# Attention and MoE on one core: two pairs of token blocks merged in the first product, w_out's landing places changed, a new written-out order

## The chip, the cores and the metric

The kernel runs on one core of a Trainium2 chip. The metric is the device time of one execution in microseconds (us). A core has five engines that run side by side, each working through its own list of instructions in order and waiting on semaphores where it needs another's result: PE (TensorE, matrix products; PEld is its loading of the stationary operand), DVE (VectorE), ACT (ScalarE), POOL (GpSimd) and SP (SyncE, which here issues the DMAs).

## The reference

```
scores = (q @ k.T) / sqrt(64)          # 4 batches, 12 heads, 448 tokens, 64 wide
attn   = softmax(causal mask(scores))  # rows divided by (sum + 1e-9)
x      = (attn @ v)                    # back to 1792 tokens x 768
h      = x @ w_in                      # 768 x 2048
g      = h * (1 / (1 + exp(-1.702 * h)))
out    = g @ w_out                     # 2048 x 768, float32
```

## The kernel before

**Numbers.** Large products are not done in float32. Each operand is split into a high and a low float16 part (`split`; `scaled` writes the high part and `rest` the low one) and three of the four products are summed: high x high, high x low, low x high. Splitting is the work of ACT and DVE. The weights arrive as int32 words and are brought to float32 first (`to_f32`), scaled by a factor from the largest sum of squares (`gram` on PE, then `gram_max`, `all_sum`, `norm_scale`), and then split. The attention of the first two groups is done in float32 (`plain=2`), that of the others in split float16.

**Blocks.** Tokens are worked in chunks of 64 columns. `TUNE["groups"]` cuts the batches into nine blocks, here numbered 0 to 8: batch 0 chunks 0-4, batch 1 chunks 0-3, batch 2 chunks 0-4 and 4-7, batch 3 chunks 0-4 and 4-7, batch 1 chunks 3-5 and 5-7, batch 0 chunks 4-7. The widths are 256, 192, 256, 192, 256, 192, 128, 128 and 192 columns. For a block and each of six head pairs u, `unit` does scores, masked exponentials (`chunk`, a custom DVE instruction), the split of p, a transposition by DMA, and the product with v, whose result lands in xT.

**The MoE of a block.** `moe(n)` follows the attention of the next block. `h_slice` computes the eight slices of w_in (256 of its 2048 columns each) for the block; both 128-column halves t of a slice share one PSUM bank, so a block may be 256 columns wide. Each slice is four PE operations of 18 matmuls (line 410, helper `halves`: a product is two matmuls of 64 weight columns that run beside each other in the array). ACT takes tanh (line 1401), DVE forms the gelu (line 1406), and gT gets the high and low parts (lines 468 and 473). `out_tile` multiplies two chunks of gT with w_out (line 1442), in two halves nh of 384 columns and eight operations of 12 matmuls each. xT and gT are rings of seven chunks.

**The weights.** w_in lands in eight slices in `wob`, whose space is later w_out's. `w_out_load` brings the 16 blocks of w_out; a block's int32 words first land in a buffer that is named in `TUNE["raw"]`: K0 is K's own staging buffer `kk`, V0 that of v (`vraw`), P0 that of p, and W11, W13, W15 are parts of `wob`.

**The order.** Nothing is scheduled at run time. Every operation is registered in `Ops.add` with the engines that may do it, and the string `ORDER` lists all of them by number and engine (S, P, A, D, G). An engine executes its operations in the order of that string, SP its DMAs too. The string is the output of a planner that worked with the cost figures in the `add` calls; those figures have no other use in the kernel.

```
    for n, (b, c0, c1, gr) in enumerate(blocks):
        ...
        if n:
            moe(n - 1)
    moe(NB - 1)
```

Of the kernel before, what the change touches and what calls it, by code (L numbers as in the profile page):

```python
# [26 lines left out]
    raw=(['W11', 'K0', 'V0', 'P0', 'W13', 'W15', 'K0', 'P0'], ['W11', 'W13', 'W15', 'V0', 'K0', 'P0', 'V0', 'P0']),  # L27
# [22 lines left out]
    wi2=2.63,  # L50
    parts=(((0, 1), (1, 3), (3, 6)), ((0, 3), (3, 6))),
# [3 lines left out]
1D 3G 2A 60S 0G 4S 45S 57S 9S 541G 14S 108S 61P 49S 5A 62A 6D 7A 84P 27S 8D 47S 58P 85A 59A 111S 10D 82P 491S 11A  # L55
46S 70P 12A 83D 13D 15A 159S 63P 71D 162S 73D 16A 109P 64D 447S 66D 74A 17D 93P 444S 72A 110D 65A 18D 86P 67A 75P
77D 96D 19P 28A 78D 94D 32S 87D 133P 89D 97A 20D 29D 79P 48S 95A 76D 21P 68P 88A 112P 22D 90A 30D 80A 98P 24D 100D
23D 113A 31D 134A 432S 121P 69A 101D 25A 99D 135P 122D 114P 124D 50S 91P 136D 123A 160P 115D 117D 125A 144P 26D 118A
436S 116A 137P 161A 163P 92A 102P 145D 164A 215S 147D 184P 146A 140D 210S 128D 148A 186P 138D 494S 129D 185D 141A
119P 103D 434S 172P 33A 187D 165P 139A 34D 81P 538S 173D 35A 168D 126P 166D 433S 175D 188P 169A 151D 120D 195P 167A  # L60
36D 174A 437S 51P 176A 191D 189D 152D 127A 196D 104P 198D 192A 52D 37P 190A 179D 228S 105D 197A 573S 53P 130P 216D
199A 545S 448P 54D 38D 217A 180D 202D 445P 56D 55D 131D 39P 149P 617D 40D 449D 106A 153P 218D 446A 42D 469P 107D
211A 142P 203D 450P 219D 150A 233S 467P 143A 435S 132P 212D 154A 470A 451D 155P 43A 213D 453D 170P 214D 177P 468A
457P 156D 452A 181P 251S 171A 41D 44D 178A 471P 193P 157A 200P 182A 454A 495P 458D 229A 204P 158D 246S 478P 194A
472D 492P 474D 459A 230D 183P 201A 479D 220P 205A 462D 231D 496A 493A 626D 324S 206P 463D 473A 232D 480A 497P 475A
504P 207D 552A 514P 221D 455P 500D 234A 498D 222P 483D 516P 505D 264S 484D 438P 223D 515A 456D 208A 235D 460P 225D
517A 439D 618P 236D 226A 209D 518P 336S 237D 440P 619P 461A 252A 224D 227D 238P 499A 501A 464P 247A 269S 525P 620P
253D 465A 635D 506A 521D 254D 476P 522A 248D 621P 553A 255D 477A 330S 325A 627P 239D 249D 622A 441D 481P 519D 250D
520A 240P 539P 482A 628P 265A 287S 443D 509D 526D 510D 241D 623D 527A 574P 629P 540A 266D 624A 243D 242D 530D 267D
244A 256P 282S 625D 630P 268D 575A 337A 485P 257D 245D 466P 631A 258P 576P 300S 487P 270A 636P 632D 486A 271A 259D  # L70
577D 502P 261D 644D 488D 637P 633A 544S 579D 272D 262A 593P 634D 638P 273D 503A 645P 288A 263D 305S 578A 639P 594A
489A 260D 274P 580A 289D 640A 531D 490D 507P 283A 646P 275D 641D 508A 290D 276P 331A 595P 284D 511P 291D 647P 301A
285D 642A 583P 277D 512A 302D 648P 596A 326A 286D 523P 643D 597P 649A 292P 279D 524A 303D 551A 654P 327D 280A 293D
304D 294P 528P 513P 295D 328D 306A 655P 297D 281D 529A 354S 298A 532P 534P 656P 307D 533A 550A 299D 581P 308A 657P
582A 338A 309D 318S 332A 278D 584D 310P 339D 585A 650D 604P 333A 311D 586P 340D 312P 651A 313D 598D 587A 588D 360S
600D 355A 315D 589D 535D 590P 652D 316A 653D 605D 663P 662D 334D 599A 601A 317D 393S 591A 319A 602P 658A 664P 320D
606A 342S 659D 603A 348S 536A 321D 607P 356A 665P 609D 296D 537D 777S 322D 660A 592P 361A 666P 661D 375S 608A 357D
362A 323P 610D 672P 671D 314D 358D 667A 611P 363D 394A 399S 673P 668D 612A 442D 680D 364D 613P 669A 674P 343A 670D
405S 329P 986D 344A 614D 675P 371D 372D 615A 349D 681P 778S 345A 616D 335P 350D 676A 682P 346D 351A 341P 677D 376A
381S 683P 352D 678A 347P 377D 684P 387S 679D 378A 400D 353P 987P 685A 379D 359P 988P 686D 395A 365P 406D 779S 989P  # L80
687D 396A 1003P 366D 688D 367P 990P 397D 995P 382A 368D 411S 370D 369D 1004P 373D 991A 374D 383D 689A 996P 992D 384D
1005P 993A 690D 780S 388A 997P 385D 1006P 691A 389D 998P 401A 407D 380P 390D 723P 999A 408D 402A 391D 386P 412A 994D
392P 403D 781A 1011P 413A 409D 398P 559S 1012P 1000D 561S 414A 404P 692D 1013P 562S 1001A 415D 410P 1007A 560S 1014P
693A 782D 1002D 417S 724P 784G 1008D 542S 783G 694D 1019P 1009A 786A 543S 1010D 416P 1015A 1020P 428D 721D 788G 787D
695A 725P 1016D 429G 859S 563A 1051D 789G 696D 1021P 856S 1017A 1348D 564P 1027P 697A 857S 1018D 565D 1022P 567D
566G 858S 698D 568A 726P 815S 785G 418D 1023A 1035P 569D 699A 1028P 790S 546A 419D 1036P 547A 700D 420A 727P 1024D
764S 549A 701D 1029P 765S 548A 421D 728P 1025A 570S 860A 702D 422P 1037P 554D 861D 1026D 703A 863G 423D 555P 729P
862D 766S 556D 558D 557G 865A 704D 424P 1043P 763S 775A 867G 425D 866D 1030P 854A 427D 426D 730P 1281D 922S 868G
776D 571A 921S 1044P 430D 855D 802P 924S 705A 791P 1038P 923S 805D 731A 1045P 706D 767A 869S 743P 803D 806A 794D
707A 792D 768P 827P 572D 732S 744P 804A 795A 816P 769D 807G 708D 1046P 793A 1191S 771G 925A 796G 745P 431D 808D  # L90
# [201 lines left out]
def kernel(  # L292
# [1275 lines left out]
```

## Time and profile before

| | |
|---|---|
| median of 3 runs | 583.18 us (582.04 to 583.66) |
| the profiled execution, its own time | 581.97 us |
| its span, first to last instruction | 580.3 us |
| PE busy | 564.2 us, 97% of the span |
| DVE busy | 424.6 us, 73% |
| ACT busy | 365.2 us, 63% |
| granted TensorE clock | 1.00 |
| DMA, mean | 149 GB/s |

The profiled execution is one run and lies near the fastest of the three timed ones. Busy shares are means over the whole span; the windows further down show that the share of DVE differs much between the first 200 us and the rest. A busy PE counts time in which a matmul is in flight, also where it goes slower than it can.

### The profile page before, as it was taken

The page shows a single profiled execution, that of the slowest core. Times are in us where ns is not written, and L with a number is a line of the kernel's source. Part 1 is how long each engine was busy: PE and PEld are TensorE (multiplying, and loading weights), DVE is VectorE, ACT ScalarE, POOL GpSimd, SP SyncE. Part 2 cuts the span into 40 slices and gives each one's busy share as a digit, 9 for nine tenths or more (in the row PEclk, how much of TensorE's full clock was granted, in tenths as well). Part 3 has the DMA queues.
Part 4 walks back from the last instruction along what each step waited for, and adds up shares of the span by engine and source line. Part 5 has one row for each costly group of instructions (what it writes and reads, how often), then busy time and mean ns, then how long its engine had stood idle before and what let it go on. Part 6 is the DMA issues. An engine that isn't in the chain of part 4 may idle for free.

```text
span 580.3 us, 24080 instructions
## 1 busy us (share of the span) xinstructions
PE 564.2 (97%) x10376; PEld 475.5 (82%) x10376; DVE 424.6 (73%) x1201; ACT 365.2 (63%) x879; POOL 60.8 (10%) x165
## 2 busy tenths in 40 slices
PE   6999979999999999999999999999999999999997
PEld 4778868988788998779977899778987978889965
DVE  3899999999998688778758759555887987823110
ACT  5899999899976566458746556364665555512210
POOL 2000000013120102101100103011102020000000
PEclk9999999999999999999999999999999999999999
DMA  8999659588997968899846967877758957620010
GB/s 267 268 275 371 199 165 334 180 190 161 187 194 152 155 124 155 141 164 170 155 71 130 154 122 111 130 157 132 119 110 141 139 97 113 107 61 3 16 28 28
DMA packets 228187, 86.70 MB, mean 149 GB/s; under 512 B 208880, under 2 KB 217840, under 8 KB 228080
## 3 DMA queue, kind: packets, MB, share of 16 engines
q1 hardware_dynamic: 228080, 85.16, 72.4%
q8 instruction: 81, 1.33, 1.0%
q14 instruction: 26, 0.21, 0.1%
HBM read 44.63 MB, written 5.51 MB: 86 GB/s over the span
## 4 chain that ended last, share of the span: by engine, by line
PE 78%; DVE 12%; DMA 4%; ACT 2%; issue 1%; SPq 1%; DVEq 0%; ACTq 0%
PE ps_o L1442 33%; PE ps_h L410 30%; PE ps_v L1302 5%; PE ps_s L1099 5%; DVE wob L592 2%; DVE wob L473 2%; PE ps_s L1090 2%; PE ps_o L913 2%; DMA wob<-in_moe_w_out_dram 2%; DMA gT<-in_k_dram 1%; PE ps_h L903 1%; DVE ps_h L1406 1%; DVE wob L558 1%; DMA out_dram<-ob 1%; DVE wob L577 1%
## 5 line engine op out<-in xcount | busy, mean ns | idle before, releaser
L410 PE MATMUL ps_h<-xT,wib 128*64 128x192 f16 (+2 forms) x5184 | 247.7, 249 | 1.2 <-DVE gT L473 0.9
L1442 PE MATMUL ps_o<-wob,gT 128*64 128x384 f16 x2688 | 237.3, 326 | 0.5 <-DVE wob L473 0.5
L410 PEld LDWEIGHTS <-wib 128*64 128x64 f16 x5184 | 224.9, 110 | 10.9 <-issue 3.2
L1442 PEld LDWEIGHTS <-gT 128*64 128x64 f16 x2688 | 153.2, 110 | 54.4 <-issue 0.9
L1136 ACT ACTIVATE z<-z,cols 128x384 f32<-128x384 f32 (+6 forms) x140 | 72.8, 521 | 56.3 <-DVE cols L1122 48.3
L1122 DVE CUSTOM_DVE_ANT_0 z<-ps_s,mask,cols 128x384 f32<-128x384 f32 (+6 forms) x126 | 62.6, 519 | 26.4 <-PE ps_s L1099 25.4
L1401 ACT ACTIVATE t<-ps_h,cols 128x384 f32<-128x384 f32 (+2 forms) x72 | 42.3, 587 | 45.8 <-PE ps_h L410 44.0
L473 DVE SCALAR_TENSOR_TENSOR p<-z,cols,p 128x384 f16<-128x384 f32 (+3 forms) x126 | 67.6, 558 | 3.4 <-ACT p L468 2.7
L1406 DVE SCALAR_TENSOR_TENSOR ps_h<-t,ps_h 128x384 f32<-128x384 f32 (+2 forms) x72 | 41.3, 574 | 37.4 <-ACT t L1401 37.0
L468 ACT ACTIVATE p<-z,cols 128x384 f16<-128x384 f32 (+3 forms) x78 | 41.7, 555 | 9.5 <-DVE cols L1262 4.9
L1099 PE MATMUL ps_s<-kT,qT 128*64 128x384 f16 (+5 forms) x504 | 45.5, 288 | 0.3 <-DMA kT<-kk 0.3
L473 DVE SCALAR_TENSOR_TENSOR gT<-ps_h,gT 128x384 f16<-128x384 f32 (+2 forms) x72 | 40.9, 567 | 6.5 <-ACT gT L468 6.3
L1302 PE MATMUL ps_v<-PT,v 128*64 128x192 f16 (+7 forms) x924 | 42.7, 237 | 0.0
L468 ACT ACTIVATE gT<-ps_h 128x384 f16<-128x384 f32 (+2 forms) x60 | 30.1, 501 | 18.1 <-DVE ps_h L1406 17.2
L468 ACT ACTIVATE ob<-ps_o,cols 128x384 f32<-128x384 f32 x24 | 13.9, 577 | 38.1 <-PE ps_o L1442 35.4
L1302 PEld LDWEIGHTS <-v 128*64 128x64 f16 x828 | 32.8, 110 | 2.1
L1256 POOL TENSOR_SCALAR cols<-cols 128x2 f32<-128x2 f32 (+1 forms) x53 | 14.4, 272 | 158.3 <-ACT z L1136 157.7
L1099 PEld LDWEIGHTS <-qT 128*64 128x64 f16 x504 | 24.5, 110 | 4.7 <-issue 0.4
L1053 POOL TENSOR_SCALAR qq<-qq 128x384 f16<-128x384 f16 (+2 forms) x32 | 20.9, 655 | 54.6 <-ACT qq L468 32.4
L1136 ACT ACTIVATION_READ_ACCUMULATOR z<-z,cols 128x1 f32 x140 | 26.5, 189 | 0.0
L449 POOL TENSOR_SCALAR cols<-cols 128x1 int32<-128x1 int32 x18 | 8.5, 470 | 164.2 <-DVE cols L435 163.9
L470 DVE TENSOR_SCALAR p<-z,cols 128x384 f16<-128x384 f32 (+3 forms) x48 | 22.8, 487 | 1.0
(121 smaller groups left out, 598.5 us busy)
## 6 DMA issues: line engine op xcount, KB each, us to landing
wob<-in_moe_w_in_dram SPq DMA_DIRECT2D x15, 768.0 KB, 7.4
kk<-in_k_dram SPq DMA_DIRECT2D x48, 112.0 KB, 3.3
vraw<-in_v_dram SPq DMA_DIRECT2D x12, 384.0 KB, 5.7
wob<-in_moe_w_out_dram SPq DMA_DIRECT2D x6, 768.0 KB, 6.5
out_dram<-ob SPq DMA_DIRECT2D x22, 192.0 KB, 2.4
p<-in_moe_w_out_dram SPq DMA_DIRECT2D x4, 768.0 KB, 7.1
kk<-in_moe_w_out_dram SPq DMA_DIRECT2D x3, 768.0 KB, 7.9
vraw<-in_moe_w_out_dram SPq DMA_DIRECT2D x3, 768.0 KB, 4.9
```

Of the source, the lines that this page charges most:

```text
L410: nc.tensor.matmul(out[o : o + 64], lhsT[:, o : o + 64], rhs, start=start, stop=stop)
L468: nc.scalar.activation(out=dst, in_=src, func=AF.Copy, scale=sc)
L470: nc.vector.tensor_scalar(out=dst, in0=src, scalar1=sc, scalar2=None, op0=ALU.mult)
L473: nc.vector.scalar_tensor_tensor(out=dst, in0=src, scalar=sc, in1=hi, op0=ALU.mult, op1=ALU.subtract)
L1053: nc.gpsimd.tensor_scalar(out=dst, in0=src, scalar1=1.0, scalar2=1.0, op0=ALU.mult, op1=ALU.mult)
L1099: nc.tensor.matmul(ps[64 * j : 64 * j + 64], qt[:, g, i - c0, 64 * j : 64 * j + 64], kt[:, : i + 1, 64 * j : 64 * j + 64], start=(g == 0), ...
L1122: lambda e: nc.vector.tensor_tensor_reduce(out=z[:, :w], in0=ps, in1=mask[:, S - w :], scale=c, scalar=3.0e38, op0=ALU.add, op1=ALU.min, a ...
L1136: lambda e: nc.scalar.activation(out=z[:, :w], in_=z[:, :w], func=AF.Exp, bias=m, scale=-1.0, accum_out=l),
L1302: nc.tensor.matmul(ps[64 * j : 64 * j + 64, 64 * (first - c0) : w], vt[:, J, j] if f32(gr) else vt[:, gv, J, j, :], (p_f32(pi)[:, at] if f ...
L1401: lambda e: nc.scalar.activation(out=th, in_=ph, func=AF.Tanh, scale=ts[:, sl : sl + 1]),
L1406: lambda e: nc.vector.scalar_tensor_tensor(out=ph, in0=th, scalar=1.0, in1=ph, op0=ALU.add, op1=ALU.mult),
L1442: nc.tensor.matmul(po[64 * j : 64 * j + 64, :OH], gT[:, r, gg, f], wo_pair(f, gw, nh), start=(f == 0 and gg + gw == 0), stop=(f == NFC - 1 ...
```

## The change

Five things are different.

- `TUNE["hb"]` groups blocks for `moe`: blocks 4 and 5 together (batch 3 whole, 448 columns) and blocks 6 and 7 together (256 columns). At 448 columns a PSUM bank holds only one half t of a slice, so `h_part` is called twice per slice. The MoE of (4, 5) is registered right after the attention of block 5, since its 448 columns of xT fill the whole ring, and block 6 writes there next.
- `TUNE["raw"]`: w_out lands in K's buffer once instead of three times; the places it leaves are taken by V0 and W15.
- The largest scale of w_in is computed once, no longer for each half of w_out (`w_in_largest`).
- `ORDER` is replaced in full.
- Cost figures that the planner used for the float32 operations are refitted, and switches are added that are off (`gram_p`, `vg`, `pt`, `zs`).

In instructions: PE has 8912 matmuls in the program instead of 10064, and as many fewer weight loads; all 1152 that go are of `h_slice` (5184 before, 4032 now). DVE has 311 to 299 TENSOR_SCALAR, 399 to 383 SCALAR_TENSOR_TENSOR, 18 to 17 TENSOR_REDUCE; ACT 645 to 638; POOL gains 3. SP's DMAs are as many as before.

```diff
-    raw=(['W11', 'K0', 'V0', 'P0', 'W13', 'W15', 'K0', 'P0'], ['W11', 'W13', 'W15', 'V0', 'K0', 'P0', 'V0', 'P0']),
+    raw=(['W11', 'K0', 'V0', 'P0', 'W13', 'W15', 'V0', 'P0'], ['W11', 'W13', 'W15', 'V0', 'W15', 'P0', 'V0', 'P0']),
...
+    hb=((0,),(1,),(2,),(3,),(4,5),(6,7),(8,)),
...
-1D 3G 2A 60S 0G 4S 45S 57S 9S 541G 14S 108S 61P 49S 5A 62A 6D 7A 84P 27S 8D 47S 58P 85A 59A 111S 10D 82P 491S 11A
...
+    parts_of = {ns[0]: ns for ns in TUNE["hb"]}
+    wide = {n: sum(blocks[x][2] - blocks[x][1] for x in ns) for n, ns in parts_of.items()}
...
     def h_slice(n, sl, prio):

-        _, c0, c1, gr = blocks[n]
-        w = 64 * (c1 - c0)
+        gr = blocks[n][3]
+        nc_ = wide[n]
+        w = 64 * nc_
         r = first_at[n] % GT
+        nt = 2 if 2 * w <= 512 else 1
+        for t0 in range(0, 2, nt):
+            h_part(n, sl, t0, nt, nc_, w, r, gr, prio + t0 / 2)
+
+    def h_part(n, sl, t0, nt, cn, w, r, gr, prio):
         hb = sl % 2 if n == 0 else ps_h_r.next()
-        ph = ps_h[hb][:, : 2 * w]
+        ph = ps_h[hb][:, : nt * w]
         half = NU // 2
-        for t in range(2):
+        for t in range(nt):
...
                             halves(
-                                ph.rearrange("p (r t x) -> p r t x", t=2, x=64)[:, :, t],
-                                wib[:, sl, u, gw, t * P : (t + 1) * P],
+                                ph.rearrange("p (r t x) -> p r t x", t=nt, x=64)[:, :, t],
+                                wib[:, sl, u, gw, (t0 + t) * P : (t0 + t + 1) * P],
...
-        if n:
-            moe(n - 1)
-    moe(NB - 1)
+        for x in range(n + 1):
+            if x in parts_of and x not in done and (parts_of[x][-1] < n or wide[x] > 4 or n == NB - 1) and parts_of[x][-1] <= n:
+                done.append(x)
+                moe(x)
```

**The start on SP.** The first DMAs that SP issues, before: q and k are loaded into `gT`, the first slice of w_in into `wob`.

```order
L894 DMA gT<-in_q_dram 128x4x128
L650 DMA wob<-in_moe_w_in_dram 128x512
L829 DMA v_69<-in_v_dram 128x4x64
L894 DMA gT<-in_k_dram 128x4x128
L650 DMA wob<-in_moe_w_in_dram 128x2x512
L650 DMA wob<-in_moe_w_in_dram 128x3x512
L894 DMA gT<-in_k_dram 128x4x128
L829 DMA v_71<-in_v_dram 128x4x64
L650 DMA wob<-in_moe_w_in_dram 128x3x512
```

The same place in the changed kernel:

```order
L659 DMA wob<-in_moe_w_in_dram 128x512
L659 DMA wob<-in_moe_w_in_dram 128x2x512
L910 DMA gT<-in_q_dram 128x4x128
L910 DMA gT<-in_k_dram 128x4x128
L845 DMA v_69<-in_v_dram 128x4x64
L910 DMA gT<-in_q_dram 128x4x128
L910 DMA gT<-in_k_dram 128x4x128
L659 DMA wob<-in_moe_w_in_dram 128x3x512
L910 DMA gT<-in_k_dram 96x4x128
```

Two parts of w_in, 256 and 512 KB, now go ahead of the first q, and the second q and k go ahead of the 768 KB that complete the slice.

**The start on DVE.** Its first operations before (L558 and L592 are steps of `to_f32`, L470 a copy, ISA is the custom instruction of `chunk`):

```order
L528 MEMSET cols 128x1
L558 TENSOR_SCALAR wob<-wob 128x256
L592 SCALAR_TENSOR_TENSOR wob<-wob 128x256
L470 TENSOR_SCALAR wob<-wob 128x512
L470 TENSOR_SCALAR kT_66<-ps_o_91 128x256
L592 SCALAR_TENSOR_TENSOR wob<-wob 128x512
L1122 ISA z,cols<-ps_s_86,mask 128x192
```

And in the changed kernel, where L601 is the line of L592, L479 that of L470 and L1138 that of L1122:

```order
L537 MEMSET cols 128x1
L601 SCALAR_TENSOR_TENSOR wob<-wob 128x256
L601 SCALAR_TENSOR_TENSOR wob<-wob 128x512
L1138 ISA z,cols<-ps_s_85,mask 128x64
L1138 ISA cols 128x1
L1138 ISA z,cols<-ps_s_85,mask 128x128
L1138 ISA cols 128x1
L479 TENSOR_SCALAR kT_66<-ps_o_91 128x256
```

Of four conversions and copies ahead of the first chunk, two are left on DVE; the first chunk is now that of 64 columns, which needs the least of k.

**K's buffer on SP.** Further on, before, the last of the three w_out blocks that land in `kk`, and the first K of batch 2 behind it:

```order
L707 DMA wob<-in_moe_w_out_dram 128x2x768
L707 DMA kk<-in_moe_w_out_dram 128x2x768
L707 DMA p_79<-in_moe_w_out_dram 128x2x768
L1010 DMA qq<-in_q_dram 64x4x64
L707 DMA wob<-in_moe_w_out_dram 128x2x768 x2
L1010 DMA qq<-in_q_dram 64x4x64
L707 DMA vraw<-in_moe_w_out_dram 128x2x768
L1010 DMA qq<-in_q_dram 64x4x64
L965 DMA kk<-in_k_dram 64x7x64 x4
```

The same place in the changed kernel:

```order
L719 DMA p_79<-in_moe_w_out_dram 128x2x768
L719 DMA wob<-in_moe_w_out_dram 128x2x768
L981 DMA kk<-in_k_dram 64x7x64 x3
L719 DMA wob<-in_moe_w_out_dram 128x2x768 x2
L981 DMA kk<-in_k_dram 64x7x64
L1026 DMA qq<-in_q_dram 64x4x64
L719 DMA vraw<-in_moe_w_out_dram 128x2x768
```

The first four K loads of batch 2 now stand ahead of seven blocks of w_out that are still to land, where they stood behind all but one.

## Rows read from the trace of the kernel before

**Rows 1.** The page: span, and busy time of each engine.

```profile
span 580.3 us, 24080 instructions
PE 564.2 (97%) x10376; PEld 475.5 (82%) x10376; DVE 424.6 (73%) x1201; ACT 365.2 (63%) x879; POOL 60.8 (10%) x165
```

**Rows 2.** The page: the chain that ended last, by engine and by line.

```profile
PE 78%; DVE 12%; DMA 4%; ACT 2%; issue 1%; SPq 1%; DVEq 0%; ACTq 0%
PE ps_o L1442 33%; PE ps_h L410 30%; PE ps_v L1302 5%; PE ps_s L1099 5%; DVE wob L592 2%; DVE wob L473 2%; PE ps_s L1090 2%; PE ps_o L913 2%; DMA wob<-in_moe_w_out_dram 2%; DMA gT<-in_k_dram 1%; PE ps_h L903 1%; DVE ps_h L1406 1%; DVE wob L558 1%; DMA out_dram<-ob 1%; DVE wob L577 1%
```

**Rows 3.** Windows: stretch, length, each engine's busy time, granted clock, DMA.

```profile
0.00:35.00 35.00, 29.39 (x398) 20.85 (x398) 23.09 (x100) 26.01 (x76) 3.09 (x19) 1.00 0.98 259
35.00:80.00 45.00, 45.00 (x838) 37.30 (x839) 44.79 (x116) 44.00 (x101) 0.00 (x0) 1.00 0.81 262
80.00:100.00 20.00, 15.97 (x316) 13.96 (x314) 19.27 (x52) 20.00 (x36) 0.00 (x0) 1.00 0.91 294
100.00:138.00 38.00, 36.53 (x850) 34.32 (x846) 37.67 (x76) 33.99 (x54) 4.54 (x11) 1.00 0.76 186
138.00:200.00 62.00, 60.54 (x912) 50.89 (x908) 54.03 (x178) 47.05 (x134) 12.72 (x30) 1.00 1.00 173
200.00:300.00 100.00, 100.00 (x1810) 86.18 (x1806) 77.79 (x238) 62.69 (x170) 13.48 (x36) 1.00 0.88 145
400.00:500.00 100.00, 100.00 (x2326) 86.59 (x2323) 79.40 (x216) 57.65 (x141) 13.33 (x35) 1.00 0.71 119
```

**Rows 4.** Timeline of PE at three places: start, length, line, tiles, count.

```profile
338.63 1.15 PE L410 MATMUL ps_h<-xT,wib 128*64 128x256 f16 x18
339.61 0.44 PE L1099 MATMUL ps_s<-kT,qT 128*64 128x320 f16 x4
...
396.83 0.91 PE L410 MATMUL ps_h<-xT,wib 128*64 128x192 f16 x18
397.58 0.59 PE L1302 MATMUL ps_v<-PT,v 128*64 128x128 f16 x18
...
448.84 0.67 PE L410 MATMUL ps_h<-xT,wib 128*64 128x128 f16 x18
449.34 0.49 PE L1099 MATMUL ps_s<-kT,qT 128*64 128x384 f16 x4
```

**Rows 5.** Timeline of PE at the start; in brackets idle before, and what ended it.

```profile
3.82 1.12 PE L913 MATMUL ps_o<-ident,gT 128*64 128x128 f32 x8 [3.82 <-DMA gT<-in_q_dram]
5.41 2.20 PE L913 MATMUL ps_o<-ident,gT 128*64 128x128 f32 x16 [0.47 <-ACT qT L468]
9.42 2.40 PE L1090 MATMUL ps_s<-kT,qT 64*64 64x192 f32 x16
15.98 0.63 PE L913 MATMUL ps_o<-ident,gT 128*64 128x128 f32 x8
```

**Rows 6.** Timeline of DVE at the start, the same columns.

```profile
4.41 0.32 DVE L558 TENSOR_SCALAR wob<-wob 128x256 uint16<-128x256 uint16 x1 [3.49 <-DMA wob<-in_moe_w_in_dram]
8.56 0.43 DVE L470 TENSOR_SCALAR wob<-wob 128x512 f32<-128x512 f32 x1 [2.37 <-DMA wob<-in_moe_w_in_dram]
11.34 0.36 DVE L1122 CUSTOM_DVE_ANT_0 z<-ps_s,mask 128x192 f32<-128x192 f32 x1 [0.65 <-PE ps_s L1090]
```

**Rows 7.** Timeline of PE from 120 to 182 us, waits of PE.

```profile
122.75 0.19 PE L414 MATMUL ps_s<-cols 128*64 128x1 bf16 x2 [0.24 <-ACT kk L458]
136.14 0.75 PE L1099 MATMUL ps_s<-kT,qT 128*64 128x192 f16 x16 [0.28 <-DMA kT<-kk]
153.44 1.00 PE L1442 MATMUL ps_o<-wob,gT 128*64 128x384 f16 x10 [0.30 <-DVE wob L473]
157.27 1.00 PE L1442 MATMUL ps_o<-wob,gT 128*64 128x384 f16 x10 [0.16 <-DVE wob L473]
181.79 0.19 PE L414 MATMUL ps_s<-cols 128*64 128x1 bf16 x2 [0.59 <-DVE cols L1122]
```

**Rows 8.** Timeline of SP: the first loads of K into `kk` for batch 2.

```profile
115.24 2.62 SPq L965 DMA_DIRECT2D kk<-in_k_dram  x4
```

**Rows 9.** Lines by form, PE: count, then busy us and mean ns of one.

```profile
L410 PE MATMUL ps_h<-xT,wib 128*64 128x192 f16 x2304 | 105.1, 246 | 0.8 <-DVE gT L473 0.5 <-issue 0.2
L410 PE MATMUL ps_h<-xT,wib 128*64 128x256 f16 x1728 | 104.7, 273 | 0.4 <-DVE gT L473 0.4
L410 PE MATMUL ps_h<-xT,wib 128*64 128x128 f16 x1152 | 37.8, 219 | 0.0
```

More of the change, by code (lines that the diff above doesn't have):

```diff
@@ L585, in to_f32 @@
         add(
[L586 removed]
+            {**dve(n, rate=0.548), **act(n, rate=1.1)},
             sign,
@@ L619, in mm @@
                     )
-        add({"PE": len(blocks) * 0.0585}, mm, [k for _, keys in parts for k in keys], ps_keys, prio)
+        add({"PE": len(blocks) * 0.036}, mm, [k for _, keys in parts for k in keys], ps_keys, prio)
     def gram_max(ps, ps_key, sq, sq_key, prio, n=64):
@@ L645, in w_in_slice @@
         src = w_in32[:, 2 * s * WS : 2 * (s + 1) * WS].rearrange("(k p) f -> p k f", p=P)
-        for x, y in TUNE["parts"][min(s, 1)]:
+        for x, y in TUNE["parts"][min(s, len(TUNE["parts"]) - 1)]:
             here, there = thirds(a, 2 * x, 2 * y), thirds(t, x, y)
@@ L749, in w_out_scale @@
         )
-        add(tiny(), lambda e: flip(e, s_x, i_x), [ix_key], [sx_key], prio)
+        add(tiny(near=True), lambda e: flip(e, s_x, i_x), [ix_key], [sx_key], prio)
+    def w_out_scale(nh, x, prio):
+        c0, c1 = TUNE["ko"][nh][x : x + 2]
+        sq, sq_key = col("sqo1", 2)
+        gram_max(*og[TUNE["og"][nh]], sq, sq_key, prio)
+        am, am_key = all_sum(sq, sq_key, "wo", og[TUNE["og"][nh]], prio)
+        (s_o, so_key), (i_o, io_key) = col("s_o", 2), col("i_o", 2)
+        norm_scale("wo", am, am_key, s_o, so_key, i_o, io_key, prio)
         add(
-            dve(NWS, ap=2),
+            dve(c1 - c0, ap=2),
             lambda e: nc.vector.tensor_scalar(
-                out=s_c[nh], in0=i_wi, scalar1=s_x, scalar2=s_o, op0=ALU.mult, op1=ALU.mult
+                out=s_c[nh][:, c0:c1], in0=i_wi[:, c0:c1], scalar1=s_x, scalar2=s_o, op0=ALU.mult, op1=ALU.mult
             ),
-            [sx_key, so_key], [("s_c", nh)], prio,
+            [sx_key, so_key] + [("i_wi", s) for s in range(c0, c1)], [("s_c", nh, x)], prio,
         )
@@ L794, in v_batch @@
         sq, sq_key = col("sqv1", 2)
+        if g in TUNE["vg"]:
+            x = ps_x_r.next()
+            ps = ps_s[x][:, XC:]
+            gram_of([(vraw.rearrange("p j h d -> p j (h d)"), [("vraw", j, h) for j in range(NJ) for h in range(2)])], ps, [("X", x)], prio)
+            gram_max(ps, ("X", x), sq, sq_key, prio)
+            v_scale(g, sq, sq_key, "X", prio)
+            return
         for j in range(2 * NJ):
@@ L1268, in unit @@
         if f32(gr):
+            if n in TUNE["pt"]:
+                p_turned(n, range(c0, c1), zx, pi, where, prio)
+        if f32(gr) and n not in TUNE["zs"]:
             la, ra = la[:, c0:c1], ra[:, c0:c1]
@@ L1321, in unit @@
         sc_keys = [bst[gr]["s_v_key"]] * ap
-        if f32(gr):
+        if f32(gr) and n not in TUNE["zs"]:
             add(
@@ L1390, in h_slice @@
                     mm,
-                    [("wi", sl, 0), ("wi", sl, 1)] + [("xT", r + x, u, g) for u in range(a, a + half) for g in range(2) for x in range(c1 - c0)],
+                    [("wi", sl, 0), ("wi", sl, 1)] + [("xT", r + x, u, g) for u in range(a, a + half) for g in range(2) for x in range(cn)],
                     [("H", hb)], 1e6 + prio + t / 2,
@@ L1475, in moe @@
     def moe(n):
-        _, c0, c1, gr = blocks[n]
+        gr = blocks[n][3]
         for s in range(NWS):
@@ L1486, in moe @@
                 out_scale(gr, nh, n * 100 + 30 - 1e6)
-        for i, tt in enumerate(range(first_at[n] // 2, (first_at[n] + c1 - c0) // 2)):
+        for i, tt in enumerate(range(first_at[n] // 2, (first_at[n] + wide[n]) // 2)):
             out_tile(tt, n * 100 + 40 + i)
@@ L1508, in keys_values @@
             v_pair(gr, u, at(n, u) - TUNE["dv"])
+    done = []
     for n, (b, c0, c1, gr) in enumerate(blocks):
```

502 lines of the change are left out of this document (269 added, 233 removed).

## The prediction

> **What bounds the kernel now.** I read the busy times first: PE is busy in 564.2 of 580.3 us, DVE in 424.6, ACT in 365.2 [rows 1]. The chain that ended last agrees, 78% of it is PE, but 12% is DVE [rows 2], so the mean hides a second limit. The windows show where. From 200 us on, PE has no idle time at all in either window of 100 us, while DVE does 78 and 79 us [rows 3]. Before 138 us it is the other way: in 35 to 138 us DVE is busy for 44.79, 19.27 and 37.67 of 103 us, idle for 1.3, and PE waits 4.0 us between 80 and 100 alone [rows 3]. In the first 35 us neither is full: PE idles 5.6, DVE 11.9.
>
> So there are two regimes. Up to about 157 us, when PE last waits for a split of w_out [rows 7], PE's lag is set by when DVE gets its work done: by DVE's idle time at the start, and by how much DVE work is listed ahead of PE's. After that the kernel is a stream of matmuls, and only their sum counts. The start itself is slow for two reasons: PE waits 3.82 us for the first q, and the same transposition of 8 matmuls takes 1.12 us at 3.82 and 0.63 at 15.98 [rows 5], though the granted clock reads 1.00 (the 2.4 GHz level) for the window.
>
> **The wider blocks.** Nine products of two matmuls each take, start to start, 0.98 us at 256 columns, 0.75 at 192 and 0.50 at 128 [rows 4], that is 109, 83 and 56 ns a product. Straight through these goes columns/2.4 plus 2.2 to 3.3 ns; I take 2.5. A block needs 8 slices x 36 = 288 products; four blocks become two, so 576 products go and their columns stay: 576 x 2.5 ns = **1.4 us less PE work**. No row shows 448 columns, so this is stretched. The least is 576 x 2.2 = 1.3; the most comes from the busy times by form, 60.6 and 32.8 ns a matmul at 256 and 128 columns [rows 9], which leave 10 ns a product, 5.8 us. I stay with the start-to-start times, since the busy time also counts the fill behind each switch between lines. ACT and DVE see the same elements in as many instructions or a few less (two of 448 for a 256 and a 192 that held both halves), which is no gain on PE.
>
> One rule speaks for a much larger gain. The rows: a product of 128 columns, two weight loads of 64 columns included, passes every 56 ns [rows 4]. The Trainium skill's TensorE: Matmul & The Clock Gate, LDWEIGHTS, gives a load its columns divided by 1.2 in ns, which is 53 for each of these and 107 for a pair in series. Products of 128 and 192 columns would then be held to 107 ns, and merging would be worth about 288 x (2 x 107 - 109) + 288 x (109 + 107 - 189) ns, an estimate of 38 us by that page. The trace disagrees: 56 ns is half of that, so the loads of the two column halves don't stand in series with each other here, and the sum stays 1.4.
>
> **The start.** In the order, q is now behind two parts of w_in, 768 KB. From the rows: by 4.41 us q and the first part, 512 KB, have landed, and by 8.56 v, k and the second part, 896 KB more [rows 6], so 216 KB per us. The 1024 KB up to and with the first q then land at 4.4 + 512/216 = 6.8, and k at 8.0. PE's first matmul moves from 3.82 to about 6.9, **3.1 us later**. But what DVE gets to do is what counts. Before, DVE's first chunk came at 11.34 [rows 6], behind 24 transposing matmuls and 16 of scores at the slow rate, 7.5 us after PE began [rows 5]. Afterwards PE has 12 program transpositions ahead of the first scores instead of 16, and the scores that come first are the two smallest. From k at 8.0: a transposition 1.1, its copy 0.8, scores about 1.2 (half of 2.40): first chunk near 11.1, and two conversions fewer ahead of it on DVE. Thereafter the second q and k are there by about 11, so the float32 scores go on without the waits that DVE had in the 11.9 idle us. I put the start at **0**. Its bounds: -1.5 (DVE's waits behind the first chunk before 35 us all go) and +3.1 (the late first matmul is carried through to the end).
>
> **DVE ahead of PE.** I added the durations of the trace along the orders of both kernels. Up to the last splits of w_out that PE waits for [rows 7], DVE's sum leads PE's by 9.7 us before; in the changed order the largest lead is 10.3. That is **+0.6**, unsure by 0.5, and it holds as long as DVE has no more idle time than before. The one computation of w_in's largest scale instead of two saves two tiny instructions; the flip that moves to DVE is one of 0.15 us, covered by the rest of DVE's queue. Both are in that sum.
>
> **K's buffer.** K of batch 2 could be loaded only when the third w_out block had left `kk`: its loads are issued at 115.24 [rows 8], and PE then waits for work on K or its transposition: 0.24 at 122.75, 0.28 at 136.14 [rows 7]. In the changed order these loads stand ahead of seven w_out blocks, and the scores of batch 2 come 4 us of PE work earlier. The 0.5 us go; the 0.59 at 181.79 is behind DVE and may go as well. What is moved past them in SP's queue is the first K load ahead of w_out blocks in `wob`; these loads wait for the one w_out block in `kk` to be converted, and everything behind on SP waits too. The next use of w_out is not before the out tiles, so that is covered; without cover it would be one w_out conversion, about 1 us. I take **-0.6**, between 0 and -1.8 (all the waits of [rows 7]: 1.6, and 0.2 beside).
>
> **The attention of blocks 3 to 5.** For (4, 5) to be multiplied together, batch 3's attention has to be complete earlier: along PE's order block 5's last product with v comes 36 us of PE work sooner, and out tiles move behind it. In the stretch from 250 to 292 us of PE work DVE has 41.2 us to do, where PE has 42; before, DVE had 78 in 100 there [rows 3]. A full DVE with nothing in reserve loses something to waits. The nearest rows: 44.79 of 45 in the window to 80 us, but 54.03 of 62 between 138 and 200 [rows 3], 87%. Added against PE's order, DVE is never behind, since it goes in with work in hand. I take **+0.4**, between 0 and 41.2/0.90 - 42 = 3.8. Where the wide h gives way to block 6, xT has to be read before it is written again; there PE has 1.7 us of other work listed against a copy and a transposition of about 1.2, so nothing.
>
> **The sum**: -1.4 + 0 + 0.6 - 0.6 + 0.4 = **-1.0 us**, from the profiled 581.97 to 581.0. That execution lies 1.2 below the median 583.18, so the median goes to **582.2**. A change of 0.3%, 1.75 us, is about what a measurement of this kernel can tell from none.
>
> **The rivals.**
>
> *The front gets shorter.* The 4.0 us that PE waits between 80 and 100 us and the 1.5 between 100 and 138 [rows 3] come from one order that put DVE and ACT at 100%. If the new order feeds w_in to DVE early and keeps it busy from 11 us, half of these (2.8) go, and the waits of K with them: -1.4 - 2.8 - 0.6 + 0.6 gives 579.0. For it: DVE has 11.9 idle us at the start. Against: the lead by sums did not shrink.
>
> *DVE becomes the bound in the batch 3 stretch.* Should it reach only 90% there, 3.8 us are lost in place of 0.4: 585.6, slower. It decides from 92%, where the loss is 2.8 and the time 584.6. For it: 87% in a mixed stretch. Against: that DVE was not asked for more there, PE was full in 60.54 of 62.
>
> *The late first matmul is carried through*: 582.2 + 3.1 = 585.3, slower. For it: PE's first 16 us are slow work. Against: DVE, not PE, was late in the 100 us after.
>
> *Merging does nothing that can be seen*: products cost only their columns, 583.6 with the rest as it is.
>
> *Weight loads bind small products*: about 545, as worked out beside that page; the rows leave it 1 in 100.
>
> **How the numbers follow.** The forecast with the fourth rival 0.40 (of it 0.36 within 0.3%, 0.04 below), the shorter front 0.36, DVE bound 0.13, late start 0.10, weight loads 0.01. That makes faster 0.41, same 0.36, slower 0.23. The likeliest is 582.2, its own range 580.5 to 584. For 8 in 10 I reach to 577.5, 1.5 below the shorter front (the upper value of the wider blocks counts there), and to 586.
>
> **What would show it.** The h matmuls of 448 columns pass 18 in 1.70 us, start to start, and PE's busy time falls by 1 to 2. The first matmul stands near 6.9 us and the first chunk near 11. No wait on `kk` is left behind 115 us. DVE's share between 250 and 300 us is above 95%, with PE full. If PE idles there, the second rival has it; if PE's idle time between 80 and 140 us falls from 5.5 below 3, the first. The forecast fails if DVE's idle time in the first 35 us changes by more than 2 us.

## The result, and the profile after

The changed kernel is slower: 591.12 us median of 6 runs (587.53 to 592.58) against 582.49 of 6 for the kernel before, ratio 1.0131 with a 95% interval of 1.0103 to 1.0160 (the quotient of the two medians alone is 1.0148). Its runs also spread over 5 us, those of before over 1.7; what makes some of them 4 us longer stays open. The profiled execution is a run of 591.62 us with a span of 589.9, 9.6 more than before; by the medians it is 8.6.

The page's busy times, and windows of the changed kernel with the columns of [rows 3]:

```profile
PE 564.1 (96%) x9224; PEld 479.5 (81%) x9224; DVE 416.4 (71%) x1171; ACT 363.7 (62%) x872; POOL 68.7 (12%) x168
```

```profile
0.00:35.00 35.00, 27.00 (x370) 19.44 (x372) 21.26 (x90) 24.20 (x72) 3.09 (x19) 1.00 1.04 273
35.00:80.00 45.00, 43.58 (x802) 35.47 (x798) 44.61 (x124) 43.79 (x104) 0.00 (x0) 1.00 0.74 233
80.00:100.00 20.00, 16.97 (x302) 14.07 (x302) 18.65 (x46) 16.58 (x32) 0.00 (x0) 1.00 0.84 232
138.00:200.00 62.00, 59.05 (x885) 50.40 (x880) 54.03 (x180) 49.36 (x135) 15.57 (x30) 1.00 0.98 158
200.00:300.00 100.00, 96.19 (x1748) 89.25 (x1746) 80.62 (x237) 65.74 (x180) 16.82 (x42) 1.00 0.87 156
300.00:400.00 100.00, 98.11 (x1290) 69.40 (x1288) 75.28 (x219) 59.70 (x150) 16.10 (x44) 1.00 0.76 136
```

The window of the kernel before that [rows 3] leaves out:

```profile
300.00:400.00 100.00, 100.00 (x1606) 82.84 (x1604) 68.87 (x190) 56.39 (x138) 13.41 (x33) 1.00 0.75 130
```

DVE and ACT are busy for less than before [rows 1], so over the whole neither grew. What is new is that PE, full from 200 to 500 us before, now has 3.8 us idle between 200 and 300 and 1.9 between 300 and 400. The timeline of PE names the longest waits there and just ahead:

```profile
177.30 0.69 PE L1344 MATMUL ps_v<-PT,v 128*64 128x256 f16 x12 [1.15 <-DMA PT<-p]
181.24 0.69 PE L1344 MATMUL ps_v<-PT,v 128*64 128x256 f16 x12 [1.27 <-DMA PT<-p]
278.75 0.75 PE L1115 MATMUL ps_s<-kT,qT 128*64 128x192 f16 x16 [2.41 <-DMA qT<-qq]
282.62 0.75 PE L1115 MATMUL ps_s<-kT,qT 128*64 128x192 f16 x16 [1.41 <-DMA qT<-qq]
381.13 0.19 PE L423 MATMUL ps_s<-cols 128*64 128x1 bf16 x2 [1.89 <-DVE cols L1138]
```

Four of the five end with a DMA, and each of these DMAs is a transposition that SP issues (of q into qT, of p into PT). The fifth is DVE, which worked without a pause from 376.63 on and had just stood still for 1.32 us until an output store had landed. That store, SP's again, was issued at 372.54:

```profile
372.54 0.73 SPq L1529 DMA_DIRECT2D out_dram<-ob  x1
376.63 0.62 DVE L479 TENSOR_SCALAR ob<-ps_o,cols 128x384 f32<-128x384 f32 x1 [1.32 <-DMA out_dram<-ob]
```

What it stores was complete at 323.35, 49 us earlier; SP's order placed it there.

To see all of the 9.6 us I took, for each operation of PE, the time from its first matmul to that of the next operation, and subtracted the usual time of its kind (0.98 us for 18 matmuls of 256 columns, for instance). What is left, in us, by stretches of the two profiled executions:

| | before | after | difference |
|---|---|---|---|
| usual times of all operations | 554.2 | 552.8 | -1.4 |
| first matmul starts at | 3.8 | 6.6 | +2.7 |
| lost in 0 to 20 us | 5.8 | 4.5 | -1.3 |
| lost in 20 to 60 | 1.3 | 2.2 | +0.9 |
| lost in 60 to 160 | 10.5 | 9.6 | -0.9 |
| lost in 160 to 400 | 0.9 | 10.5 | +9.6 |
| lost after 400 | 0.3 | 0.3 | 0 |

The split of the first 160 us depends on what is taken as usual, by about a microsecond a row. The stretch from 160 to 400 doesn't, and the whole of the loss lies there. In it PE waits for 8.6 us in all, 6.6 of them for a DMA (before: 0.6, none for a DMA). The wider blocks gave what they could, and the start and the front come out 1.4 us worse together.

Now SP's queue just ahead of the wait at 278.75, then what POOL did to the q that the late transposes carry:

```profile
263.49 5.34 SPq L797 DMA_DIRECT2D vraw<-in_v_dram  x4
268.95 4.48 SPq L981 DMA_DIRECT2D kk<-in_k_dram  x4
273.54 1.91 SPq L1026 DMA_DIRECT2D qq<-in_q_dram  x3
275.56 1.27 SPq L1084 DMA_TRANSPOSE qT<-qq  x1
276.88 0.62 SPq L1026 DMA_DIRECT2D qq<-in_q_dram  x1
277.61 1.27 SPq L1084 DMA_TRANSPOSE qT<-qq  x1
```

```profile
267.99 0.62 POOL L1069 TENSOR_SCALAR qq<-qq 128x512 f16<-128x512 f16 x1 [1.29 <-DVE cols L1301]
269.23 0.62 POOL L1069 TENSOR_SCALAR qq<-qq 128x512 f16<-128x512 f16 x1 [0.62 <-DVE qq L482]
```

The q was complete at 269.85. Its two transposes were issued at 275.56 and 277.61, because four K loads for batch 1's late part and three q loads stood ahead of the first, and one more q load ahead of the second, on SP, which had no gap there. (Adding up SP's rows from 140 to 380 us, it spends 196 of 240 us issuing before the change and 222 after; its pauses of over 0.5 us between two issues come to 32.5 us before and 3.8 after. Over the whole execution the sum is the same, 367 and 368. Of the 26 us more, 17 are more DMAs, 181 instead of 167 at their mean times of before; the other 9 are issues that take longer, those of p transposes above all, 2.67 us in the mean instead of 2.44.) And comparing, for each transposition of that stretch, its issue with the end of the last instruction that it depends on: before, 59 of them are issued 2.1 us late in the mean, 6 of them over 5 us; after, 65 are 4.0 us late, 18 of them over 5. Once issued they land as fast as before, medians of 3.3 us for qT and 5.0 for PT (3.3 and 5.1 before), so the loss is in the issue.

### The profile page after: what moved, and what is told of

Read it like the earlier page. It is cut to its first block, busy times and chain, and to the rows that moved or that the text cites. A ratio compares the mean times of both kernels' runs of the same rounds, so it can differ in the third digit from the quotient of the medians.

```text
span 589.9 us, 21743 instructions
## 1 busy us (share of the span) xinstructions
PE 564.1 (96%) x9224; PEld 479.5 (81%) x9224; DVE 416.4 (71%) x1171; ACT 363.7 (62%) x872; POOL 68.7 (12%) x168
## 4 chain that ended last, share of the span: by engine, by line
PE 73%; DVE 10%; DMA 7%; ACT 4%; issue 2%; SPq 2%; POOL 0%; DVEq 0%; ACTq 0%
PE ps_o L1496 33%; PE ps_h L419 27%; PE ps_v L1344 5%; PE ps_s L1115 5%; DVE wob L601 2%; PE ps_o L929 1%; PE ps_s L1106 1%; DMA wob<-in_moe_w_out_dram 1%; ACT waste L467 1%; DMA vraw<-in_v_dram 1%; SPq L1084 1%; DMA PT<-p 1%; DVE ps_h L1455 1%; DVE wib L482 1%; DVE gT L482 1%
## 5 line engine op out<-in xcount | busy, mean ns | idle before, releaser
L419 PE MATMUL ps_h<-xT,wib 128*64 128x256 f16 (+2 forms) x4032 | 244.8, 273 | 2.1 <-DVE gT L482 1.4
L1496 PE MATMUL ps_o<-wob,gT 128*64 128x384 f16 x2688 | 240.4, 326 | 0.2 <-DVE wob L482 0.2
L419 PEld LDWEIGHTS <-wib 128*64 128x64 f16 x4032 | 203.8, 110 | 26.5 <-issue 5.5
L1496 PEld LDWEIGHTS <-gT 128*64 128x64 f16 x2688 | 174.6, 110 | 35.2 <-issue 1.0
L1455 DVE SCALAR_TENSOR_TENSOR ps_h<-t,ps_h 128x512 f32<-128x512 f32 (+2 forms) x64 | 39.9, 623 | 54.0 <-ACT t L1450 53.8
L1138 DVE CUSTOM_DVE_ANT_0 z<-ps_s,mask,cols 128x384 f32<-128x384 f32 (+6 forms) x126 | 61.9, 516 | 18.5 <-PE ps_s L1115 18.0
L1450 ACT ACTIVATE t<-ps_h,cols 128x512 f32<-128x512 f32 (+2 forms) x64 | 40.2, 628 | 54.2 <-PE ps_h L419 52.6
L482 DVE SCALAR_TENSOR_TENSOR gT<-ps_h,gT 128x512 f16<-128x512 f32 (+2 forms) x64 | 39.6, 619 | 8.9 <-ACT gT L477 8.4
L477 ACT ACTIVATE gT<-ps_h 128x512 f16<-128x512 f32 (+2 forms) x52 | 28.2, 543 | 17.5 <-DVE ps_h L1455 17.4
L1295 POOL TENSOR_SCALAR cols<-cols 128x2 f32<-128x2 f32 (+1 forms) x51 | 18.8, 369 | 134.5 <-ACT z L1152 133.4
L601 DVE SCALAR_TENSOR_TENSOR wob<-wob 128x768 int32<-128x768 int32 (+2 forms) x24 | 22.4, 936 | 6.2 <-ACT wob L582 6.2
L1069 POOL TENSOR_SCALAR qq<-qq 128x512 f16<-128x512 f16 (+2 forms) x33 | 21.8, 664 | 32.2 <-DVE cols L1301 14.7
L479 DVE TENSOR_SCALAR p<-z,cols 128x384 f16<-128x384 f32 (+3 forms) x41 | 19.7, 497 | 7.1 <-DMA PT<-p 6.4
```

Of the source, the lines that this page charges most:

```text
L419: nc.tensor.matmul(out[o : o + 64], lhsT[:, o : o + 64], rhs, start=start, stop=stop)
L477: nc.scalar.activation(out=dst, in_=src, func=AF.Copy, scale=sc)
L482: nc.vector.scalar_tensor_tensor(out=dst, in0=src, scalar=sc, in1=hi, op0=ALU.mult, op1=ALU.subtract)
L601: lambda e: nc.vector.scalar_tensor_tensor(out=words(dst, I32, 1)[..., 0], in0=words(raw, I32, 2)[..., 1], scalar=3, in1=words(dst, I32, 1 ...
L1069: nc.gpsimd.tensor_scalar(out=dst, in0=src, scalar1=1.0, scalar2=1.0, op0=ALU.mult, op1=ALU.mult)
L1138: lambda e: nc.vector.tensor_tensor_reduce(out=z[:, :w], in0=ps, in1=mask[:, S - w :], scale=c, scalar=3.0e38, op0=ALU.add, op1=ALU.min, a ...
```

## The experiments

The theories. **Theory 1**: SP's queue. The new order packs the attention into less time, so SP has more to issue in it, and transposes that PE needs go out late. **Theory 2**: the later first matmul is carried to the end. **Theory 3**: the rate at which the DMA engines move data is the limit, not SP's issuing. **Theory 4**: the order of PE, ACT and DVE is poor in that stretch, and SP only shows it. In each diff below the lines are those of the changed kernel unless it says otherwise; ratios are to the kernel before in the same session, with 95% intervals.

**q_first.** In `ORDER`, SP's first four places:

```diff
-60S (q) and 57S (k) behind 4S and 9S (w_in)
+60S 4S 57S 9S
```

> The changed kernel with the first q and k ahead of the two parts of w_in on SP, as before the change; nothing else moves. Theory 2 (the late first matmul is carried to the end): PE starts at 3.8 us and the time falls by 2.7, to 588.4. Theory 1 (SP's queue from 140 us on, and DVE ahead of that): PE starts at 3.8, but its waits on DVE and ACT before 100 us grow by as much, and the time moves by less than 1 us.

591.65 us, ratio 1.0178 (1.0125 to 1.0231). The timeline of PE:

```profile
3.86 1.12 PE L929 MATMUL ps_o<-ident,gT 128*64 128x128 f32 x8 [3.86 <-DMA gT<-in_q_dram]
6.70 1.12 PE L929 MATMUL ps_o<-ident,gT 128*64 128x128 f32 x8 [1.71 <-DMA gT<-in_k_dram]
10.36 1.12 PE L929 MATMUL ps_o<-ident,gT 128*64 128x128 f32 x8 [2.54 <-ACT qT L477]
```

PE begins 2.7 us earlier and gives it all back by 20 us: the scores of 192 columns that start at 18.79 us in the changed kernel start at 20.01 here, behind waits for k and for ACT. Theory 2 falls.

**k_after_qT.** Four operations of SP change place:

```diff
-2086S 2089S 2088S 2087S ahead of 1563S (qT) and 1588S (qT)
+2086S 2089S 2088S 2087S behind 1588S
```

> The changed kernel with one place of SP's order altered: the four K loads of batch 1's late part (issued from 268.95 to 273.5 us, 4.5 us) go behind the two q transposes that PE waits for at 278.75 and 282.62 (2.41 and 1.41 us). Theory 1: these transposes are issued about 4.5 us earlier, the two waits (3.8 us) fall below 0.5, and the time falls by 3 to 4 us, to 587.5, if nothing behind them takes its place. Theory 3 (data rate): the transposes land as late as before, 591. Theory 2: 591.

588.01 us, ratio 1.0122 (1.0068 to 1.0176). By the clock this is not clear of the changed kernel: one run of the four took 593.6. The trace is. SP's queue in this run:

```profile
269.80 1.27 SPq L1084 DMA_TRANSPOSE qT<-qq  x1
271.12 1.07 SPq L1026 DMA_DIRECT2D qq<-in_q_dram  x1
272.29 1.27 SPq L1084 DMA_TRANSPOSE qT<-qq  x1
273.60 2.62 SPq L981 DMA_DIRECT2D kk<-in_k_dram  x4
```

The transposes go out 5.8 and 5.3 us earlier, PE has no wait for qT left, its waits from 160 to 400 us fall from 8.6 to 4.0 us and the loss there from 10.5 to 5.7, though a wait of 1.57 for PT now stands at 281. For these two waits, their place in SP's order was the cause: the same DMAs with the same bytes are issued, and SP's sum from 140 to 380 us stays at 220.

**half_the_loads**, and **before_half_the_loads** as its control. Every second load of K and Q is left out, but for the first pair of batch 2, in both kernels; so the attention works on wrong numbers, at the same times. K's line (Q's has n for g):

```diff
-lambda e, a=a, j=j: nc.sync.dma_start(
+lambda e, a=a, j=j: a and (g, u) != (2, 0) or nc.sync.dma_start(
```

> The changed kernel, leaving out every second load of K and Q after the first of batch 2 (64 of 132 DMAs; the pair's other half keeps older numbers). Theory 1 (SP's queue): about 48 us of issuing leave SP, no other engine gets more to do, the transposes go out less than 2.5 us late in the mean, the waits of PE on DMAs from 160 to 385 us (8 us) fall below 2, and the time falls by 5 to 8 us, to 583 to 586. Theory 4 (the order on PE, ACT and DVE itself is poor in that stretch, SP only shows it): less than 2 us gained. Theory 3 (data rate) also forecasts a gain here, since 5 MB fewer are moved; the next run tells it apart.

> Control: the kernel before, leaving out the same loads of K and Q. Theory 1: SP has 30 us more room there between 160 and 380 us, PE waits for DMAs 0.3 us after 138 us, so less than 1.5 us is gained, 581 to 583. A gain as large as in the changed kernel would mean that SP's queue doesn't make the difference between the two.

582.70 us, ratio 0.9998 (0.9982 to 1.0015): the whole loss comes back. The control, 581.42, gains 0.22% (0.9978, 0.9960 to 0.9997), about 1.2 us, so some 7 of the 8.4 are the changed kernel's own. (8.4 is the difference of the medians, 591.12 and 582.70, of two sessions.) SP spends 184 us instead of 222 from 140 to 380 us, the transposes are 1.6 us late, and 1.2 us are lost from 160 to 400. The same window, first of the kernel before, then of the changed one, then of this run:

```profile
160.00:380.00 220.00, 219.41 (x3723) 188.74 (x3721) 167.98 (x501) 132.89 (x345) 29.77 (x75) 1.00 0.85 143
```

```profile
160.00:380.00 220.00, 212.51 (x3367) 175.92 (x3363) 175.90 (x528) 144.71 (x394) 37.76 (x96) 1.00 0.90 156
```

```profile
160.00:380.00 220.00, 219.59 (x3473) 195.38 (x3470) 182.09 (x563) 149.99 (x408) 40.58 (x100) 1.00 0.82 145
```

The order of PE, ACT and DVE is that of the changed kernel, and PE is as full as before, with DVE and ACT doing more than in either. That order can be kept up when SP is in time. Theory 4 in its plain form falls, and with it the rival that DVE becomes the bound. Theory 3 is not told apart by this run, since fewer bytes move too, 145 GB/s here against 156.

**small_loads.** As many loads, but each with one chunk only (K's line shown):

```diff
-out=kf[64 * j : 64 * j + 64, a], in_=k[b, 2 * (u + a) + j]
+out=kf[64 * j : 64 * j + 64, a, : 1 if (g, u) != (2, 0) else NC], in_=k[b, 2 * (u + a) + j, : 64 if (g, u) != (2, 0) else S]
```

> The changed kernel with as many loads of K and Q, but each after the first of batch 2 moves only the first of its chunks (a seventh, a quarter, a third or half of its bytes; the rest of the buffer keeps older numbers). Theory 1 (the issuing on SP): each issue still takes SP about 0.6 us, so at most the longer ones get shorter, and less than half of the gain of the run with half the loads is seen, 588 to 591. Theory 3 (data rate): as good as that run or better, 582 to 586.

583.71 us, ratio 1.0023 (0.9995 to 1.0051). I had expected 588 to 591 by theory 1, so its strict form, that only the number of issues counts, is wrong. The q loads do get shorter to issue (0.62 us in the mean instead of 0.73), SP's sum falls to 212 us, the transposes are 2.9 us late, and 1.7 us are lost from 160 to 400. The sum alone doesn't decide: sp_by_need, below, has the same 212 us, and PE waits 8.1 us there from 160 to 400, 0.9 here. A transposition still lands 3.3 us (qT) and 5.0 us (PT) after its issue, so the bytes act on when it is issued, not on how long it then takes. The K and q loads themselves land sooner, in 2.1 us instead of about 3, so that part of theory 3 isn't excluded by this run.

**kv_on_act**, **late_loads_on_act**, **loads_on_act_from_185** and **k_out_on_pool** do all the work and move issues off SP. For ACT, in `v_batch` and `k_pair` (for POOL likewise in `k_pair` and `out_tile`), with the letters in `ORDER`:

```diff
-{"SP": 0.78}, lambda e, a=a, j=j: nc.sync.dma_start(
+{"SP": 0.78, "ACT": 0.78}, lambda e, a=a, j=j: (nc.sync if e == "SP" else nc.scalar).dma_start(
```

> The changed kernel, but the 64 loads of V and K for batches 2 and later are issued by ACT instead of SP; order otherwise the same. Theory 1 (SP's queue: its issuing is full from 140 to 380 us, transposes go out 4.2 us after their data are ready, 2.1 before the change): some 54 us of issuing leave SP, the mean delay of the transposes falls below 2 us, the waits of PE on qT and PT between 170 and 285 us (6.2 us in all) fall below 2, and the time falls by 4 us or more, to 587 or less, less what ACT loses by issuing 54 us itself. Theory 2 (the late first matmul, 2.7 us, is carried to the end): no change, 591. Theory 3 (the data rate of the DMA engines is the limit, not the issuing): the same bytes move, the transposes stay late, 591.

> The changed kernel, all work done, with 39 of the 64 K and V loads issued by ACT: those from 150 to 400 us whose buffer was free 3 us or more before ACT comes to the place of the load in its order, so that ACT need not wait for them. Theory 1 (SP's queue): some 32 us of issuing leave SP, the transposes go out 2 to 3 us late in the mean, PE's waits on DMAs after 160 us fall from 6.5 us to below 3, and as ACT has 40% idle there the time falls by 3 to 6 us, to 585 to 588. Theory 3 (data rate): the same bytes, 590.

> The changed kernel, all work done, with the K and V loads of the run late_loads_on_act on ACT only where SP issued them after 185 us, so that ACT, which stood still for 4.0 us before w_out's scaling at 164 us there, has none of them before. Theory 1 (SP's queue): that wait of 4.0 us goes; between 160 and 400 us the time lost against the mean pace of each kind of matmul falls from 10.5 us to 5 or 6, since the waits at 177 and 181 us stay; 585.5 to 588. Theory 4 (the order on PE, ACT and DVE is the cause, SP only shows it): 590 to 592.

> The changed kernel, but the 48 K loads and the 34 output stores are issued by POOL, which is busy for 12% of the span. Theory 1 (SP's queue): 60 us of issuing leave SP, the time falls by 4 us or more, to 587 or less, unless POOL's small scalings of cols come late behind the issues. Theories 2 (late start) and 3 (data rate): 591.

595.22 us (ratio 1.0221, 1.0180 to 1.0261), 593.03 (1.0180, 1.0132 to 1.0227), 590.14 (1.0138, 1.0119 to 1.0157) and 597.23 (1.0261, 1.0237 to 1.0286). All four miss what theory 1 forecast for the time, and 590.14 lies where theory 4 had put that run. The transposes go out about as late as in the kernel before, 1.9, 2.1, 2.4 and 1.7 us, and in kv_on_act and late_loads_on_act no wait of PE for qT or PT is left, with the bytes unchanged, which theory 3 excluded. But PE waits elsewhere. kv_on_act, then k_out_on_pool:

```profile
165.91 0.35 PE L1496 MATMUL ps_o<-wob,gT 128*64 128x384 f16 x2 [3.23 <-ACT wob L477]
```

```profile
168.07 0.21 PE L423 MATMUL ps_s<-cols 128*64 128x1 bf16 x2 [4.96 <-ACT kk L467]
```

ACT stood at a load whose buffer was not free, with w_out's scaling behind it; on POOL the K loads came late for ACT. These waits came with a lower clock besides: the granted clock falls to 0.50 (the 1.2 GHz level) for some microseconds at 168.0 us in kv_on_act, at 164.3 in late_loads_on_act and at 167.3 in k_out_on_pool, during or just behind such a wait (3.2, 4.0 and 5.0 us), and in kv_on_act 46 matmuls take 5.61 us instead of 3.93. The changed kernel, then kv_on_act:

```profile
161.17 3.93 PE L1496 MATMUL ps_o<-wob,gT 128*64 128x384 f16 x46 [0.16 <-DVE wob L482]
166.96 5.61 PE L1496 MATMUL ps_o<-wob,gT 128*64 128x384 f16 x46 [0.70 <-DVE wob L482]
```

Keeping loads off ACT until 185 us removed that wait, but PE still waits 1.8 us for PT and kT up to 183 us, 1.8 us between 274 and 281 for gT, behind an ACT that stood at a K load for 2.29 us until 271.7, and 1.6 us around 374 and 380 for the softmax. These engines have idle time, but not at those places.

The Trainium skill, DMA: Bandwidth & Descriptors, Issuing engines are not separate DMA queues, says that starting DMAs on several engines saves only the time on the sequencer that starts them, "which is usually small relative to the DMA itself". Here it is not small: issuing a q transposition takes 1.3 us of the 3.3 from issue to landing, and issuing fills 93% of SP's time from 140 to 380 us. The page also says that DMAs of several engines run on the same 16 DMA engines and interleave. In keeping with it, the q transposes land 3.8 us after their issue in kv_on_act and 4.2 in k_out_on_pool, where another engine issues beside SP (medians, against 3.3).

**sp_by_need** and **before_sp_by_need**. SP's operations from 125 to 440 us in a new order, by which of those ready is needed first by the trace, all other engines as they were; in the changed kernel 146 places change, in the one before 127.

```diff
-SP's letters of ORDER as the planner left them
+SP's letters of ORDER sorted by that rule
```

> The changed kernel with SP's DMAs from 125 to 440 us in another order, every other engine's order kept: at each step, of those whose data or buffer the trace shows ready, the one that is needed first goes next, transposes with 3 us of advantage. K loads that had 33 us to spare go behind transposes that were 6 to 15 us late. Theory 1 (SP's queue): the mean delay of the transposes from 140 to 400 us falls from 4.2 to 2 or 3 us, the waits of PE on qT, kT, PT and on v's sum (10 us between 160 and 385 us) fall below 3, and the time falls to 583 to 586. What is left over before is then the start and the front. Theory 3 (the data rate): 590. Theory 2 (late start): refuted already, the front stays as it is.

> Control: the kernel before with SP's DMAs reordered by the same rule. Theory 1: there the transposes are late by 2.1 us in the mean and PE waits for a DMA only 0.3 us after 138 us, so nothing is gained: 581.5 to 583. If it gains 3 us or more, the order of SP is poor in both kernels and doesn't explain the difference.

594.64 us (1.0190, 1.0158 to 1.0222) and 587.79 (1.0089, 1.0051 to 1.0127): both worse, and both expectations miss. In the first, the transposes are still 3.2 us late and the losses from 60 to 160 us rise from 9.6 to 15.3. A rule that puts a load off until it is just in time leaves nothing for the next delay. It shows how much hangs on SP's order in either kernel, and that a smaller sum on SP (212 us from 140 to 380) is not enough by itself; it tells the theories apart no further.

**before_late_loads_on_act**, the control to late_loads_on_act, 30 loads by the same rule in the kernel before.

> Control: the kernel before with 30 K and V loads moved to ACT by the same rule. Theory 1: the transposes are 2.1 us late there and PE hardly waits for them, so there is nothing to gain, and ACT, which is full up to 160 us, may lose: 582 to 585.

583.48 us (1.0013, 0.9990 to 1.0036). Nothing is gained there, as forecast, and nothing is lost that can be told.

## Why the prediction was wrong, point by point

- **The attention of blocks 3 to 5**, +0.4, is the step that failed, together with **K's buffer**, -0.6, which reaches the same way into the attention of batch 2. I weighed the attention that moves forward against DVE alone, and looked at SP only for the loads that were moved past others; SP's issuing stood in no term. What the runs show in its place: between 160 and 400 us PE loses 9.6 us more, most of it behind transposes that SP issues late, 1.9 behind an output store at the wide product. The rows to see it were in the trace before: SP's issuing already took 196 of 240 us from 140 to 380, with transposes 2.1 us late. 26 us more of it in that stretch left hardly a pause. The rival that was to end slower was on the right side with the wrong engine: DVE did 182 of 220 us in half_the_loads while PE was full, and in the changed kernel itself PE was full where DVE came to 95%:

```profile
284.00:318.00 34.00, 34.00 (x620) 28.47 (x616) 32.20 (x107) 24.83 (x68) 6.09 (x18) 1.00 0.83 140
```

  So the sign that was to show that rival, PE idle between 250 and 300 us, came (3.8 us) and misled: DVE's share there was 74%, not above 95%. The waits on K's buffer did go from 122 and 136 us; 0.35 us for `kk` came up at 171.9. (By SP's timeline eight blocks of w_out follow the fourth K load, not seven.)
- **The wider blocks**, -1.4: right. The usual times fall by 1.4 us, and 18 matmuls of 448 columns, which no row had shown, pass in 1.70 us, from 372.51 to the next line's 374.21:

```profile
372.51 1.87 PE L419 MATMUL ps_h<-xT,wib 128*64 128x448 f16 x18
374.21 0.39 PE L1115 MATMUL ps_s<-kT,qT 128*64 128x256 f16 x4
```

  The forecast that PE's busy time falls with it failed (564.1 after 564.2 [rows 1]): h goes from 247.7 to 244.8 us of busy time in the list of lines, but out tiles, whose work is unchanged, from 237.3 to 240.4, so the sum of busy times was not the place to look for 1.4 us.
- **The start**, 0, and **DVE ahead of PE**, +0.6: the sum is near, the mechanism right only in part. The first matmul came at 6.55 (forecast 6.9), the first chunk at 11.70 (11.1, before 11.34 [rows 6]), behind two conversions on DVE where five conversions and copies stood. But DVE was to lose its waits behind the first chunk, or at least have no more of them, and its idle time in the first 35 us rose by 1.8; PE, full from 35 to 80 us before, idles 1.4 there. Start and front to 160 us cost 1.4 us against the forecast of 0.6, and that this is so near is partly luck, since what was lost there and what was won from 80 to 138 us offset each other. q_first shows that the late start as such costs nothing.
- **The shorter front**, the rival with 0.36: PE's idle time from 80 to 138 us fell from 5.5 to 4.2, not below 3, and what was won there was lost between 35 and 80. Its chance was too high.
- **The range** ended at 586, since only one engine, DVE, was allowed to fail, for one stretch. The sum of the terms without SP was -1.0; with what it lost, -1.4 + 1.4 + 9.6 = 9.6 us of span.

What stays open: whether the number of DMAs or their bytes fill SP's time, since both cures work; whether the time comes back with all the work done, since no version of the changed kernel that did it has a median below 588; and so whether an order of all engines exists that keeps the wider blocks and beats 582 us.

## What to carry to other kernels

A queue that issues DMAs is an engine with a busy time of its own: add up its rows by stretch, and compare each issue with the moment its data were ready, before moving work forward. When one engine is full, a change that leaves all totals as they are can still cost by packing the work of another, unlisted one into less time. An experiment that takes work away can show the cause, if a control says what the same cut gives the kernel before; one that moves it to another engine may hide it, because it also puts that engine's own work late.

## What was not expected of the hardware

- An issue on SP takes 0.6 us (median) for a load of K or q, 1.3 for a q transposition and, over the whole execution, 2.5 before and 2.9 after for one of p. Between the runs the last goes from 1.8 to 2.9, also where the loads are the same, so small_loads (2.50 us in the mean against 2.62) shows no effect of the loads' size on it.
- K loads issued by ACT take it the same 0.6 us each (median, kv_on_act), v loads 0.4; on POOL a K load takes 0.7 and a store 0.6 (k_out_on_pool). In kv_on_act ACT's next operation starts at 164.92, when its load of 164.26 has been issued (0.61 us).
- PE's start 2.7 us later was free: 8 transposing matmuls took the same 1.12 us at 3.86 and 10.36 in q_first and at 9.03 in the changed kernel, 0.66 us from 17 to 18 us on in both, and the changed kernel was 1.2 us ahead by 19 us.
- A stretch at a granted clock of 0.50 came with PE's longest waits (3.2 to 5.0 us in kv_on_act, late_loads_on_act and k_out_on_pool), so such a wait cost more than its length. The clock also fell at 96.3 us in kv_on_act, where the waits ahead of it were only 1.2 and 0.7 us.
